# Gate taps on sixteen 32x32 PE tiles, PSUM pairs from any two banks, and one fixed order of all operations

## The chip, the cores and the metric

The kernel runs on one core of a Trainium2 chip. Times are device microseconds (us) of one execution. The profile lists what this kernel gives each engine: matrix multiplications on PE (4,159 recorded before the change; the 4,180 weight loads are listed as PEld), exponentials, tanh and some copies on ACT (280), maxima, products and copies on DVE (276), products and transfer issues on POOL (145), and transfer issues on SP. Its DMA shares are of 16 DMA engines. PE writes its sums to PSUM (`PS`), which the kernel declares as 128 partitions by eight banks of 512 float32 columns (`psum.tile([P, 8, 512], FP32)`).

Runs labelled slow (over 1.5% above the fastest of the same kernel) are left out of the ratios. A ratio is the mean time of one kernel's fast runs over that of the other's fast runs of the same rounds, so it is not quite the ratio of the medians quoted beside it.

## The reference

```python
def phi(x):                                   # Hedgehog features
    proj = np.einsum('bhsd,df->bhsf', x, w_phi)
    proj = proj - np.max(np.abs(proj), axis=-1, keepdims=True)
    return np.concatenate([np.exp(proj), np.exp(-proj)], axis=-1)
q_p, k_p = phi(q), phi(k)
kv  = np.einsum('bhsf,bhsd->bhfd', k_p, v)
z   = np.sum(k_p, axis=2)
num = np.einsum('bhsf,bhfd->bhsd', q_p, kv)
den = np.einsum('bhsf,bhf->bhs', q_p, z)[..., None] + 1e-06
x   = (num / den).transpose(0, 2, 1, 3).reshape(B, S, H * D)
# gated linear unit; gate_pre is a causal depthwise convolution with K = 5 taps
for k in range(K):
    gate_pre += conv_w[k][None, None, :] * xp[:, k:k + S, :]
gate = 1 / (1 + exp(-gate_pre))
out  = (gate * (x @ w_val)) @ w_out
```

There are 8 batches, 8 heads, a sequence of 576, a head size of 64 and 128 features. q, k and v are float32 and enter by DMA; the kernel works in bfloat16 and PSUM in float32.

## The kernel before

Per batch the kernel projects k and q (`kp`, `qm`, `qp`), takes maxima on DVE and exponentials on ACT (`KTIL`, `QTIL` in the profile), forms the state (`st`, `KV`), the normalised attention output (`num`, `XN`, `XT`), the gate (`gate`, then tanh on ACT into `TH`), the value product (`val`, then `GV` on DVE) and the output projection (`out`, `OUTS`). A scheduler in the kernel file simulates the engines and lists the operations in the order in which they are then issued. It also hands out PSUM banks, and a pair is always two neighbours:

```python
def find(nb):
    if nb == 2:
        for k in range(0, 8, 2):                       # pairs (0,1) (2,3) (4,5) (6,7)
            if banks[k] is None and banks[k + 1] is None:
                return k
        return None
    ...

# a read of a pair by ACT or DVE, here the exponential of k
self.nc.scalar.activation(
    self.KTIL[b % 2][:, s, c0:c0 + n, :, :].rearrange("p c a f -> p a c f"),
    self.PS[:, t.grp.bank:t.grp.bank + 2, 0:n * P].rearrange("p a (c f) -> p a c f", f=F),
    AF.Exp, scale=1.0 - 2.0 * s)
```

The gate multiplies diagonal matrices of taps with the attention output. The two parities of the sequence are stacked on the 128 partitions, so a step `j` (two heads, four steps a batch) is 12 matmuls with 128x64 weights and 288 columns:

```python
def gate(self, t, b, j):
    for s in range(3):
        for par in range(2):
            for h2 in range(2):
                h = 2 * j + h2
                nc.tensor.matmul(self.PS[h2 * D:(h2 + 1) * D, t.grp.bank + par, 0:R], self.GT[:, h, par, s, :],
                                 X[:, h, :, HALO - 8 * s:HALO - 8 * s + XH], start=(s == 0), stop=(s == 2))
```

Sixty warm-up matmuls (`WARM = 60`, on `ONES`) fill PE's idle time at the start (54 of them recorded, 17.7 us busy, from 1.5 to 38.8 us).

## Time and profile before

| | before |
|---|---|
| time | 242.62 us (median of 3, 240.5 to 244.38) |
| span of the profiled run | 239.3 us |
| PE busy | 214.5 us (90%) |
| ACT, DVE busy | 182.9 (76%), 175.8 (73%) |
| mean granted PE clock | 0.982 |

These lines are from the page of the kernel before: busy time by engine; the busy tenths and the granted PE clock in 40 equal slices; the instruction queue; the chain of work that ended last, by engine and by line; and three groups of instructions (busy us, mean ns of one | idle us just before, and what ended most of it).

```profile
PE 214.5 (90%) x4159; PEld 149.8 (63%) x4180; DVE 175.8 (73%) x276; ACT 182.9 (76%) x280; POOL 104.7 (44%) x145
...
PE   7979968788699889997899999999999999999990
...
PEclk9999979999889999999999999999999999999998
...
q8 instruction: 32, 0.52, 0.9%
...
PE 74%; DVE 8%; ACT 8%; issue 5%; DMA 1%; POOL 1%; DVEq 0%; ACTq 0%
PE PS L842 14%; PE PS L866 12%; PE PS L830 10%; PE PS L771 7%; PE PS L656 7%; PE PS L699 6%; PE PS L589 5%; ACT KTIL L673 5%; PE PS L743 4%; DVE MK L663 3%; PE PS L799 3%; PE PS L750 3%; DVE SC L577 1%; DVE GV L848 1%; DMA out_dram<-OUTS 1%
...
L673 ACT ACTIVATE KTIL<-PS 128x1024 bf16<-128x1024 f32 (+1 forms) x80 | 74.0, 950 | 10.5 <-DVE MK L663 6.0
...
L663 DVE TENSOR_REDUCE MK<-PS 128x8 f32<-128x1024 f32 (+1 forms) x40 | 44.3, 1109 | 5.0 <-PE PS L656 5.0
...
L830 PE MATMUL PS<-XT,GT 128*64 128x288 bf16 x384 | 30.3, 291 | 2.5 <-issue 2.5
```

PE is the limit: it is busy 90% of the span and makes up 74% of the chain, and the gate (L830) alone is 10% of the chain. The windows view gives PE 19.66 us of busy time out of 20 in the middle of the run (columns: length, then busy us and instruction count of PE, PEld, DVE, ACT and POOL, granted clock, DMA share, GB/s):

```profile
140.00:160.00 20.00, 19.66 (x401) 14.30 (x403) 17.64 (x30) 18.36 (x30) 10.38 (x14) 1.00 0.80 198
```

### The profile page before, as it was taken

To read this page: it belongs to the slowest core of one execution; us is meant where nothing else is said; L and a number is where in the kernel's file an instruction comes from. 1 tells how busy PE (TensorE), PEld (TensorE's weight loads), DVE (VectorE), ACT (ScalarE), POOL (GpSimd) and SP (SyncE) were. 2 spreads that over 40 slices of the span, in tenths; PEclk is the share of its full clock that TensorE was granted. 3 is DMA by queue.
4 is the path that set the end of the run, shared out by engine and by line. 5 is a ranking of instruction groups with operands and counts; after the bars stand their busy time and mean duration, and the time that the engine had idled before them with its cause. 6 is when DMAs were issued, how large, how long until landed. Compare 5 with 4: busy or idle time off the path is not lost.

```text
span 239.3 us, 9499 instructions
## 1 busy us (share of the span) xinstructions
PE 214.5 (90%) x4159; PEld 149.8 (63%) x4180; DVE 175.8 (73%) x276; ACT 182.9 (76%) x280; POOL 104.7 (44%) x145
## 2 busy tenths in 40 slices
PE   7979968788699889997899999999999999999990
PEld 2654635576485666765685777587758675785640
DVE  2399587986969868986888998898989985256310
ACT  2596865999649778995799889998999889833350
POOL 6267782173942810873047705650664170800100
PEclk9999979999889999999999999999999999999998
DMA  6899999997964999989798998565641014104335
GB/s 224 310 214 193 282 212 188 188 224 155 169 211 67 144 225 165 273 125 260 124 271 122 215 180 265 101 179 98 204 138 45 3 48 138 43 3 131 90 105 158
DMA packets 44802, 38.82 MB, mean 162 GB/s; under 512 B 29466, under 2 KB 34330, under 8 KB 44698
## 3 DMA queue, kind: packets, MB, share of 16 engines
q1 hardware_dynamic: 38400, 27.14, 45.1%
q0 software_dynamic: 6112, 11.01, 27.2%
q8 instruction: 32, 0.52, 0.9%
q10 hardware_dynamic: 250, 0.09, 0.2%
q14 instruction: 8, 0.07, 0.1%
HBM read 30.49 MB, written 9.44 MB: 167 GB/s over the span
## 4 chain that ended last, share of the span: by engine, by line
PE 74%; DVE 8%; ACT 8%; issue 5%; DMA 1%; POOL 1%; DVEq 0%; ACTq 0%
PE PS L842 14%; PE PS L866 12%; PE PS L830 10%; PE PS L771 7%; PE PS L656 7%; PE PS L699 6%; PE PS L589 5%; ACT KTIL L673 5%; PE PS L743 4%; DVE MK L663 3%; PE PS L799 3%; PE PS L750 3%; DVE SC L577 1%; DVE GV L848 1%; DMA out_dram<-OUTS 1%
## 5 line engine op out<-in xcount | busy, mean ns | idle before, releaser
L687 POOL TENSOR_TENSOR VT<-VN,EK 128x1152 bf16<-128x1152 f32 x32 | 67.8, 2118 | 73.8 <-ACT EK L681 73.8
L673 ACT ACTIVATE KTIL<-PS 128x1024 bf16<-128x1024 f32 (+1 forms) x80 | 74.0, 950 | 10.5 <-DVE MK L663 6.0
L758 ACT ACTIVATE QTIL<-PS 128x1024 bf16<-128x1024 f32 x64 | 64.3, 1033 | 3.0 <-PE PS L750 2.8
L663 DVE TENSOR_REDUCE MQP<-PS 128x8 f32<-128x1024 f32 (+1 forms) x40 | 43.7, 1113 | 12.2 <-PE PS L656 12.2
L663 DVE TENSOR_REDUCE MK<-PS 128x8 f32<-128x1024 f32 (+1 forms) x40 | 44.3, 1109 | 5.0 <-PE PS L656 5.0
L842 PE MATMUL PS<-XT,WV 64*128 64x288 bf16 x512 | 37.9, 288 | 0.6 <-ACT KTIL L673 0.3
L848 DVE SCALAR_TENSOR_TENSOR GV<-TH,PS 128x576 bf16<-128x576 bf16 x32 | 24.0, 750 | 16.0 <-PE PS L842 15.1
L830 PE MATMUL PS<-XT,GT 128*64 128x288 bf16 x384 | 30.3, 291 | 2.5 <-issue 2.5
L866 PE MATMUL PS<-WOUT,GV 128*128 128x512 bf16 x114 | 31.3, 381 | 0.7
L842 PEld LDWEIGHTS <-WV 64*128 64x128 bf16 x512 | 25.8, 95 | 6.5 <-issue 2.7
L834 ACT ACTIVATE TH<-PS 128x576 bf16<-128x576 f32 x32 | 21.0, 657 | 10.2 <-PE PS L830 10.2
L830 PEld LDWEIGHTS <-GT 128*64 128x64 bf16 x384 | 19.2, 109 | 9.7 <-issue 6.9
L699 PE MATMUL PS<-VT,KTIL 64*128 64x65 bf16 x1152 | 22.0, 193 | 2.1 <-issue 1.8
L699 PEld LDWEIGHTS <-KTIL 64*128 64x128 bf16 x1152 | 20.6, 96 | 5.2 <-issue 2.6
L791 DVE TENSOR_TENSOR XN<-PS,RCP 128x512 bf16<-128x512 f32 x32 | 22.1, 691 | 1.2 <-DVE RCP L788 0.2
L589 PE MATMUL PS<-ONES 128*128 128x512 bf16 x54 | 17.7, 453 | 1.6 <-DVE ONES L493 1.5
L771 PEld LDWEIGHTS <-QTIL 128*128 128x128 bf16 x512 | 17.1, 98 | 3.0 <-issue 1.8
L771 PE MATMUL PS<-KV,QTIL 128*128 128x65 bf16 x512 | 18.4, 194 | 0.5 <-DVE MK L663 0.5
L656 PE MATMUL PS<-W,kT 64*128 64x128 bf16 x288 | 15.1, 217 | 4.0 <-DVE KV L707 2.2
L656 PE MATMUL PS<-W,qT 64*128 64x128 bf16 x288 | 14.7, 217 | 4.4 <-ACT KTIL L673 2.4
L713 ACT ACTIVATE OUTS<-PS 128x512 f32<-128x512 f32 x17 | 10.2, 599 | 9.3 <-PE PS L866 8.6
L866 PEld LDWEIGHTS <-GV 128*128 128x128 bf16 x128 | 11.0, 98 | 10.0 <-issue 0.4
(70 smaller groups left out, 249.1 us busy)
## 6 DMA issues: line engine op xcount, KB each, us to landing
out_dram<-OUTS SPq DMA_DIRECT2D x32, 256.0 KB, 3.1
VN<-in_v_dram SPq DMA_DIRECT2D x7, 1152.0 KB, 6.5
KQN<-in_k_dram POOLq DMA_DIRECT2D x7, 576.0 KB, 8.1
KQN<-in_q_dram POOLq DMA_DIRECT2D x7, 576.0 KB, 6.4
KTIL<-in_k_dram SPq DMA_DIRECT2D x4, 288.0 KB, 4.0
VN<-in_v_dram POOLq DMA_DIRECT2D x1, 1152.0 KB, 18.1
KTIL<-in_q_dram SPq DMA_DIRECT2D x4, 256.0 KB, 4.1
out_dram<-OUTS SPq DMA_DIRECT2D x16, 64.0 KB, 2.9
```

Of the source, the lines that this page charges most:

```text
L589: self.nc.tensor.matmul(self.PS[:, t.grp.bank, :], self.ONES[:, 0:P], self.ONES[:, :], start=True, stop=True)
L656: nc.tensor.matmul(self.PS[:, t.grp.bank + par, i * P:(i + 1) * P], X[rows, (c0 + i) * P:(c0 + i + 1) * P], self.W2[rows, :], start=True, ...
L663: self.nc.vector.tensor_reduce(o, self.PS[:, t.grp.bank:t.grp.bank + 2, 0:n * P].rearrange("p a (c f) -> p a c f", f=F), AX.X, ALU.max, ap ...
L673: self.nc.scalar.activation(self.KTIL[b % 2][:, s, c0:c0 + n, :, :].rearrange("p c a f -> p a c f"), self.PS[:, t.grp.bank:t.grp.bank + 2, ...
L687: nc.gpsimd.tensor_tensor(self.VT[g][:, s, :, 0:D], self.VN[b % 2][:, NC * g:NC * g + NC, :], e.to_broadcast([P, NC, D]), ALU.mult)
L699: nc.tensor.matmul(self.PS[:, t.grp.bank + ab, (s * 2 + x) * E1:(s * 2 + x + 1) * E1], self.KTIL[b % 2][rows, s, J // 2, J % 2, :], self.V ...
L758: self.nc.scalar.activation(o, i, AF.Exp, scale=1.0 - 2.0 * s)
L771: nc.tensor.matmul(self.PS[:, t.grp.bank + h // 4, (h % 4) * E1:(h % 4 + 1) * E1], Q[:, s, c % 2, h, (c // 2) * P:(c // 2 + 1) * P], self. ...
L830: nc.tensor.matmul(self.PS[h2 * D:(h2 + 1) * D, t.grp.bank + par, 0:R], self.GT[:, h, par, s, :], X[:, h, :, HALO - 8 * s:HALO - 8 * s + X ...
L842: nc.tensor.matmul(self.PS[:, t.grp.bank + par, 0:R], self.WV2[rows, h, j * P:(j + 1) * P], X[rows, h, :, HALO:XW], start=(h == 0), stop=( ...
L848: nc.vector.scalar_tensor_tensor(out=self.GV[b % 3][:, j, :, :], in0=self.TH[j][:, :, :], scalar=1.0, in1=self.PS[:, t.grp.bank:t.grp.bank ...
L866: nc.tensor.matmul(self.PS[:, t.grp.bank, :], lhsT, self.WOUT[:, j, :], start=(j == 0), stop=(j == 3))
```

## The change

The change wants a shorter gate, fewer PSUM stalls and a better order. It has four parts.

1. A pair of gate steps becomes 80 matmuls of 32x32 tiles, on sixteen tile positions (`tile_position` below). Weights, the value weights and `VT` change their layout to match.
2. A pair of PSUM banks may be any two banks, read with a strided slice.
3. The scheduler is gone. Tables hold an order found by annealing (`ORDER`, 991 operations), the engine of movable operations (`FLEX`) and the banks (`BANKS`).
4. Smaller moves: `EK` is one step a batch instead of two, some copies change between ACT and DVE, and 5 warm-up matmuls stay of 60.

```diff
-WARM = 60
+WARM = ("11:7:5")
+ORDER = ("0 23 1 3 19 24 27 2 25 7 4 33 5 20 9 21 40 28 11 10 ...")      # cut
+BANKS = ("124141200534674501672727352325674523535012735274654627405713...")  # cut
+    def two(self, g, n):
+        a, b = g.banks
+        return self.PS[:, a:b + 1:b - a, 0:n]
     def kexp(self, t, b, u, s):
-            self.PS[:, t.grp.bank:t.grp.bank + 2, 0:n * P].rearrange("p a (c f) -> p a c f", f=F),
+            self.two(t.grp, n * P).rearrange("p a (c f) -> p a c f", f=F),
...                                       # the same in kmax, qmax, qexp, kv, nrm, tanh, gv
-    def gate(self, t, b, j):
...
+    def gate(self, t, b, jj, part, gs):
+        if part == 0:
+            seq = [((1, 1, s), (0, 0, s)) for s in range(3)]
+        else:
+            seq = [((0, 1, s), (1, 0, s + 1)) for s in range(2)]
+        seq = [x for pair in seq for x in pair]
+        if part == 1:
+            self.nc.tensor.drain()
+        for i, (c, par, s) in enumerate(seq):
+            for db in range(2):
+                for q in range(4):
+                    o = (db + q) % 2
+                    h = 4 * jj + 2 * o + q // 2
+                    rows = slice(32 * (2 * c + db), 32 * (2 * c + db) + 32)
+                    nc.tensor.matmul(self.PS[32 * q:32 * q + 32, gs[o].banks[par], 0:R],
+                                     self.GT[rows, h, 4 - (2 * s + par - c), :],
+                                     X[rows, h, :, HALO - 8 * s:HALO - 8 * s + XH], ...,
+                                     tile_position=(32 * (2 * c + db), 32 * q))
```

The table holds 240 pairs of banks; 56 are neighbours, the other 184 are two to seven banks apart.

## The prediction

> **What bounds the kernel now.** The chain of work that ended last is 74% PE, 8% DVE, 8% ACT; PE is busy 90% of the span. The windows show three regimes. From 120 to 200 us PE is busy 19.5 of every 20 us, ACT 18.0 to 18.8, DVE 17.5 to 18.6: a batch takes 23.4 to 24 us (repeat of the chain's pattern), set by PE, with ACT only about 2 us behind. From 20 to 120 us PE is busy 86.5 of 100 us: stalls on ACT exponentials, DVE maxima and weight preparation. From 200 us on only PE matters.
>
> **What the change removes.** Before, a gate step is 12 matmuls of 128x64 weights and 288 columns; the timeline shows 0.86 us from start to start of the next work, four a batch: 3.44 us, 27.5 us in all; the chain has 9.6% (23 us) on that line. After, a pair of steps is 80 matmuls of 32x32 tiles[...]. Against that: 160 weight loads and matmuls a batch instead of 48, two drains[...]. Closest in the trace are the sixteen 32-row transposes (0.23 us, 14 ns each[...]) and the state matmuls (72 in 1.19 us, 16.5 ns each). [...]gain 1.2 to 1.5 us per batch, 10 to 12 us in all, if PE stays the limit.
>
> **What it adds or moves.** EK: four ACT instructions of 239 ns a batch become two; KV copies move from ACT (14 to 5) to DVE, output evictions from DVE (19 to 14) to ACT. Summed, ACT loses some 5 us and DVE about none. VT on POOL becomes four instructions for two (2.12+0.26 us now; estimate 2.5 to 2.8): POOL has slack. PSUM pairs from any banks and the fixed order remove stalls, mostly in the first 120 us: I expect 3 to 6 us there. Weight preparation is shorter (two POOL operations of 2.77 us and ten small DVE copies go). The tail gains 1.5 to 3 us from its last two batches' gates.
>
> **Limit afterwards.** From start-to-start times I estimate per batch: PE about 21.2, ACT 21.4, DVE 20.1 us. Three engines are nearly level, so not all of PE's gain shows: I expect 22 to 22.4 us a batch instead of about 24.
>
> **Predicted: 223 us, 8 in 10 between 214 and 232; faster by over 2%: 0.94, within 2%: 0.04, slower: 0.02.**
>
> **What would show it.** A pair of gate steps in 0.9 to 1.1 us start to start (before 2 x 0.86). PE's busy time falls by 10 to 17 us (warm-up matmuls fall from 60 to 5). Chain: PE's share falls to 60 to 70%, ACT's and DVE's together rise above 16%. ACT is busy over 95% in the middle. The windows from 20 to 120 us hold more work than before.
>
> **What would make it wrong.** If the 32x32 pairs go at 16 ns or more, gates take over 2.8 us a batch and gain 6 us at most. If the drain costs over 0.4 us, likewise. If the fixed order was fitted to durations that the chip does not show, in-order engines wait on each other: the gain shrinks to 5 us. If the order packs ramp and tail better than I think, below 214. Fewer warm-up matmuls could lower the granted clock in the first 20 us.

The gate's term, 1.2 to 1.5 us a batch and 10 to 12 us in all, stays as the author's estimate. With 3 to 6 us for stalls and 1.5 to 3 us for the tail, the gains named come to 14.5 to 21 us (13 to 18 us if the tail is part of the gate's). Taken from 242.62 us, they leave 221.6 to 228.1 us (224.6 to 229.6 us); the forecast is 223 us. The two measured rates, 14 and 16.5 ns, would give 2.24 to 2.64 us a batch for 160 pairs, a gain of 0.8 to 1.2 us.

## More of the kernel before

A difference between two experiments of different rounds compares medians taken on different chips, so a few us of it may be noise: the kernel before has medians of 241.63, 242.68, 243.39 and 246.4 us in the four sets of the experiments.

ACT, which reads PSUM for the exponentials, sat idle only 10.5 us before all 80 exponentials of k.

## The result

The changed kernel is correct and takes **457.12 us** (median of 4 runs, 455.57 to 458.41), against 241.7 us (4 runs, 240.5 to 244.38) for the kernel before. The ratio is 1.893, with a 95% interval from 1.881 to 1.905. All four runs of the changed kernel were fast ones; of the other four, the highest lies 1.6% above the lowest.

The same lines of the page after (without the chain, which accounts for only some 2% of the span in this profile, so the prediction about its shares cannot be checked):

```profile
PE 278.1 (61%) x5003; PEld 184.9 (41%) x5021; DVE 185.9 (41%) x283; ACT 187.6 (41%) x259; POOL 106.3 (23%) x203
...
PE   7754355557655666567556757676665555565783
...
PEclk9865555556555655595565796988895885579898
...
q8 instruction: 39, 0.64, 0.6%
...
L530 ACT ACTIVATE KTIL<-PS 128x1024 bf16<-128x1024 f32 (+1 forms) x80 | 73.7, 941 | 94.9 <-DVE MK L520 16.1
...
L520 DVE TENSOR_REDUCE MK<-PS 128x8 f32<-128x1024 f32 (+1 forms) x40 | 44.5, 1114 | 43.9 <-ACT KTIL L530 12.9
...
L700 PE MATMUL PS<-XT,GT 32*32 32x288 bf16 x1280 | 25.8, 352 | 17.4 <-DVE MQP L520 5.0
```

No single operation of ACT or DVE became slow. An exponential of k takes 941 ns against 950 before, a maximum 1114 ns against 1109. ACT and DVE are busy for 188 and 186 us, much as before, but spread over 454 us. What grew is idle time: ACT now waits 94.9 us before the exponentials of k (10.5 before). The new releaser is odd: the exponential waits most for a DVE maximum, and the maximum waits most for an exponential. PE has gaps everywhere, and its granted clock is at 0.5 in long stretches; here is the window that stands above, for the changed kernel:

```profile
140.00:160.00 20.00, 12.33 (x191) 6.83 (x189) 6.41 (x9) 7.22 (x8) 0.00 (x0) 0.59 0.14 40
```

The timeline of the changed kernel shows the pattern (start us, duration us, engine, line, operation, count, and in brackets the idle time before it and its releaser):

```profile
180.80 0.76 DVE L719 SCALAR_TENSOR_TENSOR GV<-TH,PS 128x576 bf16<-128x576 bf16 x1 [4.75 <-PE PS L713]
181.59 1.02 ACT L530 ACTIVATE KTIL<-PS 128x1024 bf16<-128x1024 f32 x1 [3.94 <-DVE GV L719]
181.61 0.28 PE L713 MATMUL PS<-XT,WV 64*128 64x288 bf16 x1 [0.92 <-DVE GV L719]
...
182.66 1.14 PE L713 MATMUL PS<-XT,WV 64*128 64x288 bf16 x15 [0.78 <-ACT KTIL L530]
...
183.81 0.76 DVE L719 SCALAR_TENSOR_TENSOR GV<-TH,PS 128x576 bf16<-128x576 bf16 x1 [2.25 <-PE PS L713]
184.61 1.04 PE L630 MATMUL PS<-KV,QTIL 128*128 128x65 bf16 x16 [0.81 <-DVE GV L719]
```

The DVE operation at 180.80 reads banks 1 and 4. The exponential at 181.59 reads banks 2 and 7, has no bank in common with it, and yet starts when it ends. The first value matmul at 181.61 writes bank 1 and really had to wait for that DVE read. The second, at 182.66, writes bank 4, which the DVE read had also left at 181.56; but it starts when the exponential over banks 2 and 7 ends. Bank 4 is not one of the two; it lies between them. The DVE operation at 183.81 then reads banks 0 and 3 and waits for these matmuls into 1 and 4.

So the theory is: the read `PS[:, a:b+1:b-a, ...]` of banks a and b is recorded by the framework's dependency tracking as an access to the whole stretch from a to b. I counted this in the compiled programs, without the chip: for each wait of PE, ACT or DVE on another of the three that names a PSUM access, I compared the banks that both really touch. A recount, which attributes a wait on a group of operations in two other ways, gave 424 or 486 for the changed kernel and 723 or 806 for e1 below, and none before and in e2: the exact number depends on the way of counting, the pattern does not.

| program | waits with a common bank | waits with none (only in between) |
|---|---|---|
| before | 761 | 0 |
| after | 296 | 479 |

That a wait without a common bank protects nothing in PSUM was not shown by itself; e2 and e5 below are correct without these waits.

Three rivals were open: the chip might be slow when it reads banks that lie apart; the annealed order might not fit the chip's durations; and the 32x32 gate might be the cost.

### The profile page after: what moved, and what is told of

Its sections match the earlier page's. It is cut to its first block, busy times and chain, and to the rows that moved or that the text cites. A ratio compares the mean times of both kernels' runs of the same rounds, so it can differ in the third digit from the quotient of the medians.

```text
span 454.1 us, 11226 instructions
## 1 busy us (share of the span) xinstructions
PE 278.1 (61%) x5003; PEld 184.9 (41%) x5021; DVE 185.9 (41%) x283; ACT 187.6 (41%) x259; POOL 106.3 (23%) x203
## 5 line engine op out<-in xcount | busy, mean ns | idle before, releaser
L530 ACT ACTIVATE KTIL<-PS 128x1024 bf16<-128x1024 f32 (+1 forms) x80 | 73.7, 941 | 94.9 <-DVE MK L520 16.1
L546 POOL TENSOR_TENSOR VT<-VN,EK 128x288 bf16<-128x288 f32 (+1 forms) x90 | 72.2, 828 | 144.4 <-ACT EK L538 121.3
L713 PE MATMUL PS<-XT,WV 64*128 64x288 bf16 x512 | 52.9, 364 | 16.1 <-ACT KTIL L530 4.3
L520 DVE TENSOR_REDUCE MK<-PS 128x8 f32<-128x1024 f32 (+1 forms) x40 | 44.5, 1114 | 43.9 <-ACT KTIL L530 12.9
L713 PEld LDWEIGHTS <-WV 64*128 64x128 bf16 x512 | 34.8, 120 | 29.1 <-issue 19.5
L630 PE MATMUL PS<-KV,QTIL 128*128 128x65 bf16 x512 | 27.9, 223 | 15.3 <-ACT QTIL L617 3.7
L602 PE MATMUL PS<-qT,W 64*128 64x512 bf16 (+1 forms) x80 | 23.7, 480 | 21.6 <-ACT KTIL L530 8.8
L700 PE MATMUL PS<-XT,GT 32*32 32x288 bf16 x1280 | 25.8, 352 | 17.4 <-DVE MQP L520 5.0
L630 PEld LDWEIGHTS <-QTIL 128*128 128x128 bf16 x512 | 25.1, 117 | 22.0 <-issue 20.7
L648 DVE RECIPROCAL RCP<-PS 128x8 f32<-128x8 f32 (+1 forms) x40 | 8.1, 202 | 51.0 <-ACT QTIL L617 13.8
L513 PEld LDWEIGHTS <-kT 64*128 64x128 bf16 x288 | 13.1, 115 | 35.6 <-issue 34.9
L700 PEld LDWEIGHTS <-GT 32*32 32x32 bf16 x1280 | 13.4, 92 | 28.9 <-issue 26.9
```

What stands on the lines that cost most here:

```text
L513: nc.tensor.matmul(self.PS[:, t.grp.banks[par], i * P:(i + 1) * P], X[rows, (c0 + i) * P:(c0 + i + 1) * P], self.W2[rows, :], start=True, ...
L520: self.nc.vector.tensor_reduce(o, self.two(t.grp, n * P).rearrange("p a (c f) -> p a c f", f=F), AX.X, ALU.max, apply_absolute_value=True)
L530: self.nc.scalar.activation(self.KTIL[b % 2][:, s, c0:c0 + n, :, :].rearrange("p c a f -> p a c f"), self.two(t.grp, n * P).rearrange("p a ...
L546: eng.tensor_tensor(self.VT[g][:, s, j:j + 9, o:o + n], self.VN[b % 2][:, NC * g + j:NC * g + j + 9, i:i + n], e[:, j:j + 9, :].to_broadca ...
L602: nc.tensor.matmul(self.PS[:, t.grp.banks[par], 0:n * P], self.W2[rows, :], X[rows, c0 * P:(c0 + n) * P].rearrange("p (y h x) -> p h y x", ...
L630: nc.tensor.matmul(self.PS[:, t.grp.banks[h // 4], (h % 4) * E1:(h % 4 + 1) * E1], Q[:, s, c % 2, h, (c // 2) * P:(c // 2 + 1) * P], self. ...
```

## The experiments

Twelve kernels were run. In the first set the runs of the kernel before were uneven: one took 498.36 us, and it and four others of the seven were labelled slow (the four at 244.58 to 249.52 us), so ratios of that set rest on few runs.

### e1: the kernel before, only its banks renamed

Bank k becomes bank k/2 + 4 (k mod 2), so each pair (k, k+1) becomes two banks at a distance of 4. Order, operations and gate stay.

```diff
+def M(k):
+    return k // 2 + 4 * (k % 2)
-            self.PS[:, t.grp.bank:t.grp.bank + 2, 0:n * P].rearrange("p a (c f) -> p a c f", f=F),
+            self.PS[:, M(t.grp.bank):M(t.grp.bank) + 5:4, 0:n * P].rearrange("p a (c f) -> p a c f", f=F),
```

> The kernel before with its banks renamed only: each pair that was k, k+1 becomes k, k+4; order, gate and table untouched. Theory (a strided two-bank access is tracked as if it covered the banks between, so engines wait for accesses to banks they do not touch): clearly slower than 242 us, over 300 us, with waits of ACT and DVE on each other and a granted clock under 0.9, while single reads keep their durations (exponential of 1024 elements 1.03 us, maximum 1.22 us). Rival (the fixed order, or the 32x32 gate): within 2% of 242 us, because neither is in it. Rival (reading two banks far apart is slower on the chip): slower, with longer single reads.

Measured: 640.91 us (637.86 to 645.19), ratio 2.610 [2.585, 2.635], correct. Its page:

```profile
PE 363.4 (57%) x4159; PEld 232.3 (37%) x4180; DVE 185.1 (29%) x276; ACT 197.5 (31%) x280; POOL 104.8 (16%) x145
...
PEclk9585555555585555755558555765557556585589
...
L677 ACT ACTIVATE KTIL<-PS 128x1024 bf16<-128x1024 f32 (+1 forms) x80 | 75.0, 938 | 157.1 <-PE PS L846 30.3
```

The old kernel, with the old order and the old gate, is slower than the changed one as soon as its pairs lie apart. An exponential takes 938 ns on average (950 with neighbours), so the read of far banks is not slow in itself. The expectation held. Its program has 784 waits without a common bank.

### e2: the changed kernel, only the bank table redrawn

The order leaves room for pairs (0,1), (2,3), (4,5), (6,7) throughout: I found a table by colouring the lifetimes with backtracking.

```diff
 BANKS = (
-    "124141200534674501672727352325674523535012735274654627405713..."
+    (all 240 pairs now two neighbours, first bank even; ORDER and FLEX unchanged)
```

> The changed kernel, same fixed order and engines for every operation, but the table of banks redrawn so that every pair is 2k, 2k+1. Theory (false waits from strided pairs): the loss goes, 215 to 235 us, clock over 0.95, PE busy over 85%. Rival (the fixed order is unsuited to the chip): stays over 400 us. Rival (32x32 gate slow): stays far over 242 us with the time on the gate line.

Measured: 264.71 us (263.56 to 268.37), ratio 1.0759 [1.0655, 1.0864], correct; no wait without a common bank is left (0 of 776). So 192 us of the 215 us lost go with the table alone. The theory's own range (215 to 235 us, clock over 0.95, PE busy over 85%) was missed all the same: the clock is 0.899, and

```profile
PE 210.3 (80%) x5003; PEld 147.3 (56%) x5021; DVE 182.4 (69%) x283; ACT 180.3 (69%) x259; POOL 107.8 (41%) x203
```

In order of such waits the programs are e2 (0, 265 us), after (479, 457 us) and, from the kernel before (0, 242 us), e1 (784, 641 us): which comes to 0.40 us (192 / 479) and 0.51 us (399 / 784) for each.

But e2 is still some 22 us slower than before, although it has the shorter gate. Its waits of PE (us in total, times, longest us):

```profile
PE PS L700 <- issue: 11.1, 7, 3.8
PE PS L513 <- DVE MQP L520: 4.3, 8, 0.9
```

"issue" means that PE waited for nothing that the profile shows. Over all lines PE has 14.9 us of this in e2; the kernel before has 4.7 us, 2.5 of it at its gate.

### e5: the changed kernel, far pairs read in two halves

Table and order are those of the changed kernel. Only each read of two banks that are not neighbours is split into two reads of one bank.

```diff
+    def parts(self, g):
+        a, b = g.banks
+        return [(0, 2, a)] if b - a == 1 else [(0, 1, a), (1, 2, b)]
-        self.nc.scalar.activation(..., self.two(t.grp, n * P)...)
+        for p in self.parts(t.grp):
+            self.nc.scalar.activation(... [:, p[0]:p[1]], self.at(p, n * P)...)
```

> The changed kernel with its own table of banks and its own order; only each read of two banks that are not neighbours becomes two reads of one bank each, so no wait can name a bank between. Theory (false waits): from 457 us down to 255 to 285 us, although ACT and DVE get about 20 instructions a batch more each[...]. Rival (this choice of banks or this order is bad by itself): stays over 350 us.

Measured: 268.43 us (267.44 to 270.09), ratio 1.112 [1.1002, 1.1239], correct, and within the expected range. The banks are as scattered as in the changed kernel and more instructions read them, and the time falls by 189 us. It is not the place of the banks, it is the strided form of the access.

### e3 and e4: what is left of the loss: gate, or order

e3 is e2 with the old gate of 12 matmuls a step, and the old layouts with it, in the same places of the new order. e4 is the kernel before, with its scheduler and neighbour pairs, and only the new gate.

```diff
 # e3 against e2
-        for i, (c, par, s) in enumerate(seq):      # 80 matmuls of 32x32 in two parts
-            ...
+        j = 2 * jj + part                          # 12 matmuls of 128x64 a part
+        for s in range(3):
+            ...
```

> The run with redrawn banks, but each gate step as the 12 matmuls of the kernel before, in the same places of the order, with the weights and values laid out as before. If the 16-tile gate saves what was predicted (1.2 to 1.5 us a batch) and PE sets the time, this is 8 to 12 us slower than the run with redrawn banks; if other engines set it, under 5 us slower; if the 32x32 gate is the slow part, it is faster.

> The kernel before with its own scheduler and aligned pairs, and only the gate done by 32x32 tiles (a gate now opens two pairs at once). If the gate gain is real and shows: 230 to 236 us. If its four banks at once starve the other operations: 238 to 250 us. If the 32x32 gate is the cause of the 457 us: far slower.

Measured: e3 251.9 us (250.22 to 255.11), ratio 1.0231 [1.0119, 1.0342]. e4 264.97 us in its only fast run, 264.97 to 278.9 in four. Both say the same: with the new gate the kernel is 13 us slower in the new order (e2 against e3), and in the old order it is slower than before by some 20 us (its one fast run, and a scheduler that now has to place other blocks of work), so the new gate gains in neither. For e3 the third branch of the expectation came true; e4 lies outside all its three ranges. In e4 the profile (of a slow run, so only the kind of wait counts here) shows where:

```profile
PE PS L672 <- issue: 9.3, 1, 9.3
PE PS L716 <- issue: 7.6, 1, 7.6
```

Neither line is the gate. Whatever PE was doing, it stood still for 9.3 us and waited for nothing shown. In e2 it stopped inside a gate step:

```profile
120.37 1.37 PE L700 MATMUL PS<-XT,GT 32*32 32x288 bf16 x52
125.57 0.70 PE L700 MATMUL PS<-XT,GT 32*32 32x288 bf16 x28 [3.83 <-issue]
```

The trace also has the transfers of the instruction queue (q8 on the page): 32 of them before, 39 after and in e2, 16,384 bytes each. One of them started at 123.32 us in e2, in the middle of this pause, and landed at 124.30; from 119 to 126 us the DMA engines were full with loads of the next batch (packets took 108.9% of the 16 engines' span, 0.9% of it this queue's). That gave a second theory: the changed kernel has 1,685 more PE instructions than the one before (10,024 loads and matmuls recorded in place of 8,339; its gate alone has 1,792 more, and 55 warm-up matmuls went), PE's instructions arrive in blocks over the DMA engines, and PE sometimes runs out of them while a block waits behind loads. The counts fit it: 8,339 recorded instructions to 32 transfers and 10,024 to 39 are 261 and 257 for each. How such a block is fetched no trace shows.

### e6 and e7: lighter loads, wrong results on purpose

e6 is e2, e7 is e3, with most of q, k and v not loaded from batch 2 or 3 on, and fewer blocks in the transposing transfers from batch 4 on.

```diff
+        if b >= 3:
+            o, i = (o[:, :, 0:D], i[:, :, 0:D]) if w == "k" else (o[:, 0:4 * D], i[:, 0:4 * D])
-            ... self.N[w][b][:, :, :] ...
+            n = NC if b < 4 else 2
+            ... self.N[w][b][:, 0:n, :] ...
```

> Wrong results on purpose: the run with redrawn banks, but from the third or fourth batch on the loads of q, k and v move a ninth of their data and the transposing DMAs two blocks of 18 from the fifth batch on. Theory ([...]fetching them waits behind the loads): the stalls of PE that wait for nothing shown (15 us in the run with redrawn banks) fall under 6 us, nearly all before the lighter loads begin, and the time falls by more than 8 us. Rival (the drain or the 32x32 mode itself is slow): PE's stalls at the gate stay.

> Wrong results on purpose: the same lighter loads in the run with redrawn banks and the old gate. It gains less than the run with the new gate does. Theory: with light loads the new gate wins by 3 to 8 us where it lost 13 us with full loads. Rival: the old gate still wins by over 5 us.

Measured: e6 250.1 us (248.2 to 252.34), e7 250.86 us (248.73 to 251.38). With less load traffic the new gate's version falls by 14.6 us, the old gate's by 1.0 us. With the light loads the new gate was expected to win by 3 to 8 us; it wins by less than 1 us, so that part failed. The gate's waits on nothing in e6 fall to

```profile
PE PS L707 <- issue: 4.6, 6, 1.4
```

from 11.1 us. Over all lines they fall from 14.9 to 6.0 us, the edge of what was expected, and of the six longer than 1 us three come after the loads were lightened, against the expectation. So the 13 us that the new gate costs are an interaction of the gate with the loads. Where the loads are light the two gates tie.

### e8, e11 and e12: more PE instructions without 32x32 tiles

These cut the old 128x64 gate matmuls by columns: e8 in two (96 load and matmul pairs a batch instead of 48), e11 in four (192; the 32x32 gate has 160), both in the kernel before; e12 is the cut in four in e3. Sums and layouts are the same.

```diff
-                for h2 in range(2):
-                    nc.tensor.matmul(self.PS[..., 0:R], self.GT[:, h, par, s, :], X[:, h, :, HALO - 8 * s:HALO - 8 * s + XH], ...)
+                for k in range(4):
+                    for h2 in range(2):
+                        x = HALO - 8 * s + k % 2 * (XH // 2)
+                        nc.tensor.matmul(self.PS[..., k * (XH // 2):(k + 1) * (XH // 2)], self.GT[:, h, par, s, :],
+                                         X[:, h, k // 2, x:x + XH // 2], ...)
```

> The kernel before, with every gate matmul of 288 columns cut into two of 144: [...]same banks and order, 96 instead of 48 weight-load and matmul pairs per batch. If more PE instructions alone make PE wait for their fetch: 3 to 10 us slower, with PE's waits for nothing shown rising from 4.7 us. If only 32x32 tiles or the drain matter: within 2% of the kernel before, those waits unchanged.

> The kernel before with each gate matmul of 288 columns cut into four of 72: 192 pairs of weight load and matmul a batch in place of 48, which is more than the new gate's 160, with the same sums, the old weight layout, the old order and the old banks; 2304 more PE instructions than before, 1685 in the changed kernel. If it is the number of instructions, fetched in blocks behind the loads, that stops PE, its instruction packets rise to about 41 and waits of PE on nothing rise from 4-5 us to 10 us or more, and the time to 248-258 us. If it is something of the 32x32 tiles[...], these waits stay under 6 us and the time within 3% of before.

> The same cut in the version with neighbour pairs, the new order and the old gate (251.9 us, 2.7 us of such waits). By number of instructions: waits on nothing of 8-15 us and 258-268 us, like the version with the new gate (264.7). By the tiles: within 4 us of 251.9.

Measured: e8 243.54 and 243.24 us in its fast runs, ratio 1.0077 [0.993, 1.0224], within noise, and its waits on nothing are 4.2 us (4.7 before): by its own expectation e8 spoke for the tiles and against the number of instructions. e11 and e12 repeat the test with a larger dose. e11 257.5 and 259.89 us in its fast runs (261.93 us median of four, two slow), against 241.03 to 241.63 us of the kernel before. e12 274.81 us (272.77 to 275.71), ratio 1.138 [1.1296, 1.1464]. All are correct. e11 is at the upper edge of its range, e12 some 7 us above its own, so the direction was right and the size too small. The waits of PE in e11:

```profile
PE PS L832 <- issue: 5.5, 4, 3.6
PE PS L771 <- issue: 4.4, 1, 4.4
PE PS L656 <- issue: 3.9, 2, 3.7
PE PS L844 <- issue: 3.2, 2, 2.3
```

The gate's own work hardly grew: in quiet stretches a cut step still takes 0.9 us from its start to that of the next work (142.20 to 143.10 us; 0.86 before). The instruction queue has 41 packets, and PE waits on nothing for 18.6 us over all lines (17.0 in the four shown), where the kernel before has 4.7; in e12 it is 19.2 us, in e3 3.1 (the 2.7 of the expectation is its largest line). One step shows the same broken form as e2:

```profile
151.14 0.48 PE L832 MATMUL PS<-XT,GT 128*64 128x72 bf16 x18
155.22 1.11 PE L832 MATMUL PS<-XT,GT 128*64 128x72 bf16 x30 [3.60 <-issue]
```

What settles it is the place of the pauses. I numbered all of PE's records of e11 in the trace from 0: weight loads, matmuls and the few semaphore and drain records between them. Between 40 and 230 us it has eight gaps of over 1 us from one start to the next, before numbers 961, 1729, 2241, 3009, 3265, 4289, 5825 and 9409. Every one of them is 193 more than a multiple of 256. In e12 the same holds for all eight such gaps from 65 to 240 us; the earlier gaps of both runs wait for DVE, ACT or a load. In e5, which has the new gate and whose trace is complete, all nine such gaps on nothing are again 193 more than a multiple of 256. In e4, from whose trace a few records are missing, the two pauses of 9.3 and 7.6 us lie before numbers that are both 187 more than a multiple of 256. PE pauses at one fixed place in every 256 instructions, as it would where blocks of that size end, with old and new gate alike.

And in each of these sixteen gaps of e11 and e12, and also in the two of e4 and the one shown of e2, PE starts again 1.2 to 1.6 us after a block of the instruction queue has landed; in e4 those blocks started only 7.3 and 5.3 us after PE had stopped. So it is the number of PE instructions, not the tiles. The kernel before has three such pauses too, of 1.2 to 2.0 us. The dose matters: 768 more (e8) did nothing visible, 2,304 more (e11) cost some 17 us (258.7 against 241.3 us, the means of the fast runs).

### e9 and e10: the clock at the start

In e2 and e3 the granted clock is 0.50 from 20 to 40 us, where the kernel before has 1.00 and 0.83, and the last `GV` of batch 0 starts at 78.0 and 78.1 us against 72.65 (the expectations call this the end of batch 0). The natural reason is the warm-up matmuls, 5 instead of 60. e9 (e2) and e10 (e3) have 58 more.

```diff
-    "11:7:5"
+    "11:7:5 21:3:2 26:6:2 35:2:2 46:3:3 50:1:3 55:6:3 61:3:3 64:3:3 75:4:3 78:4:3 "
+    "84:0:2 93:6:4 102:2:3 110:6:3 121:1:3 135:4:5 140:5:3 149:6:2 157:0:3 175:0:3"
```

> The neighbour-pair version of the changed kernel (264.71 us) with 58 more warm-up matmuls, set into the first 175 places of its order, so 63 in place of 5 (the kernel before has 60). If the low granted clock of 20 to 40 us (0.50, against 1.00 and 0.83 before) is what its start loses, the clock there rises to above 0.8, the end of batch 0 moves from 78.0 us to 73-75, and the time falls by 3 to 5 us, to 259-262 us. Rival, the start is bound by loads and by the vector and scalar engines and the clock only follows PE's idleness: the clock rises but the time stays within 1.5 us of 264.7. The later stalls of PE that no wait explains stay in both, at 10 to 15 us.

> The same 58 more warm-up matmuls in the version with the old gate (251.9 us). If the clock at the start is its loss, the time falls to 247-249 us and the end of batch 0 moves from 78.1 us to 73-75; if all that is left between it and the kernel before is this start, it comes to within 2% of before. Rival: within 1.5 us of 251.9.

Measured: e9 266.24 us (265.09 to 274.6), ratio 1.1032 [1.0902, 1.1161]; e10 256.44 us (255.14 to 258.56), ratio 1.0637 [1.053, 1.0744]. The windows of e2, then of e9:

```profile
20.00:30.00 10.00, 8.20 (x94) 6.33 (x91) 5.85 (x12) 7.71 (x13) 6.89 (x11) 0.50 1.21 207
30.00:40.00 10.00, 7.08 (x131) 5.63 (x130) 7.54 (x10) 7.86 (x10) 7.25 (x11) 0.50 0.85 145
```

```profile
20.00:30.00 10.00, 8.29 (x109) 5.19 (x110) 7.87 (x14) 8.46 (x14) 4.09 (x7) 1.00 1.21 191
30.00:40.00 10.00, 7.36 (x93) 4.12 (x91) 7.25 (x9) 8.29 (x12) 9.90 (x15) 1.00 0.79 156
```

In e9 the clock rose to 1.00 and bought nothing: the last `GV` of batch 0 starts at 79.7 us there and at 83.3 in e10 (where the clock is 1.00 from 20 to 30 us and 0.69 from 30 to 40), later than without. e9 takes 1.5 us more than e2, as its rival said; e10 is 4.5 us slower than e3, which neither branch expected. So my remedy for the start fails. The test is not a clean one: at 0.25 us each (three in 0.74 us), an estimate from the timeline of e10, 58 warm-up matmuls take some 14 us of PE's own time, so a gain from the clock and a loss from this work could cancel. In e10 PE's longest wait at the start is one of 5.9 us (5.2 us in e3),

```profile
PE PS L513 <- DVE qT L496: 5.9, 1, 5.9
```

and the DVE timeline shows that DVE was then busy with ten small tap copies of the old gate's weight preparation (7.06 us together, one of them 2.0 us), which stand ahead of that transposed-q copy in the new order. What the start of e2, which has fewer such copies, waits for instead was not separated. That the low clock in e2 and e3 was a sign of an idle PE rather than the cause of the late start fits this, but is not shown.

No version that was run beats the kernel before.

## Why the prediction was wrong

**The step that failed** is "PSUM pairs from any banks and the fixed order remove stalls, mostly in the first 120 us: I expect 3 to 6 us there." Freer pairs were costed as a gain of up to 6 us. They cost about 190 us: 192 us go when only the table is redrawn (e2), 189 us when only the form of the read changes (e5), and the same form alone takes the kernel before from 242 to 641 us (e1). The strided slice over two banks is tracked as all banks from the first to the last, and 479 waits in the program follow from accesses that share no bank. I had read `two()` in the diff and asked whether it gives the right data, not what it orders. The compiled program was at hand before the prediction, so its waits could have been compared then. The prediction's own warning, that in-order engines might wait on each other, named the symptom; it put it down to wrong durations and priced it at a smaller gain.

**The gate's term was mis-sized.** Predicted were a gain of 1.2 to 1.5 us on the 3.44 us of a batch, and 0.9 to 1.1 us for a pair of steps. Undisturbed, in e6, the 80 matmuls take 1.21 us from start to start (186.61 to 187.82 us):

```profile
186.61 1.28 PE L707 MATMUL PS<-XT,GT 32*32 32x288 bf16 x80
187.82 0.39 PE L609 MATMUL PS<-qT,W 64*128 64x512 bf16 x2
```

That is 2.4 us a batch, 15 ns for each load and matmul pair. Five rounds of sixteen in 1.21 us are 0.24 us a round. In the kernel before, 16 value matmuls of the same 288 columns take 0.98 us to the start of the next work (56.68 to 57.66 us), so sixteen of the small tiles pass in a quarter of that time. The 1.21 us include the drain, which was not measured apart. It is one reading of several: where other work stands between the two parts of the gate in e6, the first 48 matmuls take 0.66 to 0.91 us and the last 32 mostly 0.40, so a pair of steps costs about 1.1 to 1.3 us. The gain is an estimated 1.0 us a batch (3.44 less 2.42), or 8 us in all (some 7 to 10 over that range), before the pauses. The closest operations that the prediction named took 14 and 16.5 ns each, and the measured 15 lies between the two. The gain that I predicted leaves 1.94 to 2.24 us a batch, 12 to 14 ns a pair: an estimate that no trace showed.

**What the prediction did not have at all** is the price of PE instructions as bytes. 39 blocks instead of 32 pass over DMA engines that are busy in the first half (in e2 a mean share of 0.88 up to 120 us, 0.59 to 1.05 in each 20 us), and PE pauses at one place in every 256 instructions (e5, e11, e12): 11.1 us of waits on nothing at e2's gate. This takes more than the gate gains (e2 against e3: 13 us slower; e11: some 17 us slower with no new tile in it).

**The limit afterwards was wrong with it.** I expected three nearly level engines, ACT above 95% busy in the middle. ACT is busy 36% in the window from 140 to 160 us (7.22 of 20), because the engines take turns.

**PE's busy time** was to fall by 10 to 17 us. It rose from 214.5 to 278.1 us, while the mean granted clock fell from 0.982 to 0.691: the same matmuls took longer (364 ns for one of the value product, 288 before). In e2 it is 210.3 us, 4.2 us less than before, although most of the 17.7 us of warm-up matmuls (L589) went.

**The warning about the clock** came true as a reading (0.50 from 20 to 40 us in e2), but more warm-up gave nothing back (e9, e10).

**Still open.** With light loads both gates stand at 250 to 251 us, some 8 us above the kernel before. The gate is excluded as the cause (e7 has the old one). What is left is what e3 and e7 keep of the change: the order, the engines of the movable operations, the table of banks, the single `EK` step and the 5 warm-up matmuls. Some 5.4 us are there by the last `GV` of batch 0 in e3; which choice costs them was not separated. The gain that I expected from the annealed order (part of 3 to 6 us) was not seen in any version.

## What to carry to other kernels

An access pattern is also a claim about dependencies: before a buffer is read with a stride, check in the built program which other buffers its waits name. Here 479 of 775 waits named no shared bank, and the strided form alone took the kernel before from 242 to 641 us. Many small matmuls can be quicker in their own place and still lose by their number: here a pair of gate steps went from 1.72 to 1.21 us (e6), for seven more instruction blocks and 13 us more in all (e2 against e3). If PE pauses "on nothing" while DMA is full, number its records: here the pauses came at one place in every 256, and PE went on 1.2 to 1.6 us after an instruction block had landed (e2, e4, e11, e12). A low granted clock next to idle PE time need not be the cause: in e9 the clock from 20 to 40 us rose from 0.50 to 1.00, and the time by 1.5 us. Added warm-up matmuls test this only in part, for they take PE time themselves (an estimated 14 us for 58).
